# An attention and mixture-of-experts kernel: weight differences, token sums and outputs at other places

## Chip, core and metric

One core of a Trainium2 chip. The metric is the device time of one execution in microseconds (us). The engines are TensorE (PE; its weight loads, which overlap it, are PEld), VectorE (DVE), ScalarE (ACT), GpSimd (POOL) and SyncE (SP), which here only issues DMAs, all from one queue in order.

## The reference

Three stages over 4 x 576 = 2304 tokens: block-causal attention (8 heads of 64), an expert with h·cos(h), and eight experts with weights from eight rounds of normalisation. The groups of this change are those of the last stage:

```
def _moe2_ref(x, w_gate, w1, w2):          # x 2304x512, w1 8x512x1024, w2 8x1024x512
    logits = x @ w_gate; logits = logits - logits.max()
    P = np.exp(logits)
    for _ in range(8):
        P /= P.sum(1, keepdims=True) + 1e-09
        P /= P.sum(0, keepdims=True) + 1e-09
        P *= N / E
    for e in range(E):
        h = np.maximum(x @ w1[e], 0.0)
        out += P[:, e:e + 1] * (h @ w2[e])
    return out
```

## The kernel before

Every product in fp32 is made of three matmuls (`mm3`, L521 to L524) from "high" and "low" halves: a high half is a rounded copy (ScalarE), the low one the rest (VectorE or GpSimd subtracts the high half from the source). In the row names below, `xh`/`xl` and `wah`/`wal` are such halves.

The experts' stage works through 96 groups: three blocks of 768 tokens, in each 32 groups (8 experts by 4 slices of the hidden width). The first product of a group, x by a slice of w1, is made in seven products of sums of quarters instead of eight plain ones (the quarters' and sums' names are A11 to A22, S1 to S4 for one side, B11 to B22, T1 to T4 for the other). TensorE writes them to the PSUM tiles `hx`, `hy` and `hz`; copies and additions `c[0]`, `c[1]`, `c[2]` put them together.

*First block (groups 0 to 31).* These groups also make what the later blocks reuse. `wload` (L590) loads the slices of w1 and w2 of two groups on into two tiles `stg`. `Weights` then makes sums of w1's quarters on GpSimd (`s`, L603 to L606), high halves on ScalarE (L612, L613), low halves on VectorE (L617, L619), halves of w2 (`v`, ScalarE and GpSimd, L636, L637), and stores w1's halves to DRAM (L643). `differences` (L650) makes the four sums of quarters of w2 in place in `stg`, in two parts of two subtractions on VectorE, and the second part issues their store to DRAM (`td`, L654). In these groups the second product, h by w2, is six plain outputs (`y`, tile `acc`), one group later: y(0), y(1) behind product S3, y(2) to y(5) at the end. While groups 1 to 5 run, VectorE also makes the eight rounds of P (`plan`).

*Later blocks (groups 32 to 95).* Groups go in pairs (`Pair`, `pair_group`). The second product of a pair is made in seven products too: X1, Y1, X2, Z, X3, Y2, X4, each over three token tiles, 21 items. `TURN` is their order; X1 uses A11 by B11, Y1 uses S1 by T1, X2 uses S2 by T2, Z uses A12 by B21. `items(n)` runs n of them between the seven first products of the pair that follows. `high` (ScalarE) and `low` (L1113, VectorE) split the hidden side, `both` (L1122, L1125) makes its sums, `w2_split` (ScalarE L1077, GpSimd L1078) splits the side of the weights that came from DRAM. The six outputs of group 31 are made in group 32, in the slots of the pair that isn't there yet.

*The token sums.* `tprep` (L658) makes T1 to T4 of the next block: nine additions of 128 x 768 on GpSimd (L665), with T1's split in their middle; T2 to T4 are split in the last group of a block. `sums(n)` goes n steps further; it starts nine groups ahead of a block's end and goes on at each group's end, one step in even groups and two in odd ones.

The order on every engine is the order of the code.

Of the kernel before, what the change touches and what calls it, by code (L numbers as in the profile page):

```python
# [10 lines left out]
F32 = mybir.dt.float32  # L11
# [10 lines left out]
N, DM = B * S, H * D  # L22
# [4 lines left out]
TB = 384  # L27
# [5 lines left out]
NJ = F2 // 2  # L33
# [10 lines left out]
def attention_moe_kernel(ctx: ExitStack, tc: tile.TileContext, qk, v, w_a, gate, w_b, out):  # L44
    nc = tc.nc
# [26 lines left out]
    raw = [None] * F1  # L72
# [76 lines left out]
    post = ctx.enter_context(tc.tile_pool(name="post", bufs=2))  # L149
# [367 lines left out]
    with tc.manual_schedule():  # L517
# [53 lines left out]
        groups = [(tb, e, j) for tb in range(N // HB) for e in range(NE) for j in range(NJ)]  # L571
        NG, NA = len(groups), NE * NJ
        stg, wa, wv = {}, {}, {}
        drw = ctx.enter_context(tc.tile_pool(name="drw", bufs=1, space=bass.MemoryType.DRAM))
        W1D = [drw.tile([128, 14 * HK], F32, name=f"w1d{g}") for g in range(NA)]
        TD = [drw.tile([128, 4, 2, HK], F32, name=f"td{p}") for p in range(NA // 2)]
        PARTS = ((0, 3 * HK), (3 * HK, 3 * HK), (6 * HK, 4 * HK), (10 * HK, 4 * HK))
        th = tl = None

# [12 lines left out]
        class Weights:  # L592
# [40 lines left out]
            def v(self, i, eng=nc.gpsimd):  # L633
                src = stg[self.g][i][:, DM:2 * DM]
                t = wp.tile([128, 2 * DM], F32R, tag="w", name="wv")
                nc.scalar.activation(t[:, 0:DM], src, AF.Copy)  # L636
                eng.tensor_tensor(out=t[:, DM:2 * DM], in0=src, in1=t[:, 0:DM].bitcast(F32), op=ALU.subtract)  # L637
                wv[self.g, i] = t

            def store(self):  # L640

# [2 lines left out]

            def differences(self, part, eng=nc.vector):

                a, b = (t[:, DM:2 * DM] for t in stg[self.g])
                b11, b12, b21, b22 = a[:, 0:HK], a[:, HK:2 * HK], b[:, 0:HK], b[:, HK:2 * HK]
                for out, in0, in1 in (((b11, b12, b11), (b12, b12, b22)), ((b22, b22, b11), (b21, b21, b22)))[part]:
                    eng.tensor_tensor(out=out, in0=in0, in1=in1, op=ALU.subtract)  # L650
                if part:
                    p, k = divmod(self.g, 2)
                    for i, t in enumerate((a, b)):
                        nc.sync.dma_start(out=TD[p][:, 2 * i:2 * i + 2, k, :],  # L654
                                          in_=t.rearrange("p (o n) -> p o n", n=HK))
                    stg.pop(self.g)

        def tprep(tb, eng):  # L658

# [281 lines left out]
        fin = ctx.enter_context(tc.tile_pool(name="fin", bufs=1))  # L941
# [132 lines left out]
        def w2_split(p, o):  # L1074
            if (p, o) in W2:
                t, raw = W2[p, o], raws.pop((p, o))
                nc.scalar.activation(t[:, 0:DM], raw, AF.Copy)  # L1077
                nc.gpsimd.tensor_tensor(out=t[:, DM:2 * DM], in0=raw, in1=t[:, 0:DM].bitcast(F32), op=ALU.subtract)  # L1078
                w2_load(raw)
# [6 lines left out]
                ("Z", 0), ("Z", 1), ("X3", 0), ("X3", 1), ("X3", 2), ("Y2", 0), ("Y2", 1), ("Z", 2),  # L1086
                ("X4", 0), ("X4", 1), ("X4", 2), ("Y2", 2)]

        class Pair:


            def __init__(self, p):
                self.p = p
                self.tb, self.e, self.j = groups[2 * p]
                self.raw, self.h, self.l, self.bank, self.todo = {}, {}, {}, {}, list(TURN)

            def get(self, o, k=None):
                if o not in self.raw:
                    tag = places.pop(0)
                    self.raw[o] = tag, fin.tile([128, 2, TB], F32, tag=tag, name="raw")  # L1100
                r = self.raw[o][1]
                return r if k is None else r[:, k]

            def drop(self, o):
                places.append(self.raw.pop(o)[0])

            def high(self, o):
                self.h[o] = halves.pop(0)
# [54 lines left out]
                if self.e == NE - 1 and self.j == NJ - 2 and name in ("Y2", "X4"):  # L1163
                    nc.sync.dma_start(out=out[r * 128:(r + 1) * 128, :], in_=oa[r])

        def pair_group(g, old, new, splits, ys):

            k, now = g % 2, g < NG
            p = g // 2
            x = yy = c = None  # L1170

            def items(n):
                if old:
                    for _ in range(n):
                        old.multiply()
                elif k == 0:
                    for _ in range(n):
                        ys()

            if now:  # L1180
                c = [fin.tile([128, TB], F32, tag=f"c{i}", name="c") for i in range(3)]
# [13 lines left out]
            if old and k == 0:  # L1195
                old.low("S1")
                w2_split(p - 1, "B21")
            elif old:
                w2_split(p - 1, "T4")
            items(2)  # L1200
            if old and k == 0:
                old.both("S2", "A22", "S3", ALU.add)
# [32 lines left out]
                nc.vector.tensor_tensor(out=new.get("A22", k), in0=yy, in1=c[2], op=ALU.add)  # L1235
                splits("T3")
            if old and k == 0:
                old.low("A12")
            if now and k:
                new.low("A11", True)  # L1240
                w2_split(p, "T1")
            items(2)
            if now:
                product(g, x, "A22", "T4", False)
                nc.scalar.activation(new.get("A12", k), x, AF.Relu)
                splits("T4")
                if k:
                    new.relu("A22")
            if old and k == 0:
                old.high("S3")  # L1250
                old.high("S4")
                old.low("S3")
                w2_split(p - 1, "B22")
            items(1)
            if now:
                product(g, yy, "S4", "B22", False)
                nc.vector.tensor_tensor(out=new.get("A21", k), in0=yy, in1=c[1], op=ALU.add)
                if k:
                    new.high("A12")
                    w2_split(p, "T2")  # L1260
            items(2 - k)
            if now and k:
# [16 lines left out]
        tgen, at = None, ""  # L1279
        pairs = {}  # L1280
        used = {(2 * (NA - 1) + i) % 3 for i in range(2)}
        places = [f"hs{i}" for i in range(6) if i % 3 not in used]
        rest = list(range(2 * TT))

        def last_ys():
# [5 lines left out]
        for g in range(NG + 2):  # L1291
            now, w = g < NA, Weights(g + 1) if g + 1 < NA else None
            left = NE * NJ - g % (NE * NJ)
            if left == 9 and g + 9 < NG:
                tgen = tprep(groups[g + 9][0], nc.gpsimd)
                at = "sum"

            def sums(n):
# [10 lines left out]
            if g >= NA:  # L1309
                p = g // 2  # L1310
                if g == NA:
                    more = fin.tile([128, 4 * HK], F32, tag="s", name="s")
                    w2_load(more[:, 0:DM])
                    w2_load(more[:, DM:2 * DM])
                    w2_load(post.tile([128, S], F32, tag="lt", name="raw", bufs=1)[:, 0:DM])
                if 2 * p < NG and p not in pairs:
                    pairs[p] = Pair(p)
                pair_group(g, pairs.get(p - 1), pairs.get(p), splits, last_ys)
                sums(1 + g % 2)
                continue  # L1320

            def ys(t):
                if g:
                    y(g - 1, t)
# [5 lines left out]
            if now:  # L1330
# [23 lines left out]
                    w.lo_b()  # L1354
                product(g, x, "S3", "T3", False)
                gate("S3")
                Weights(g).differences(0)
                nc.scalar.activation(c[2], x, AF.Copy)
                nc.vector.tensor_tensor(out=c[2], in0=yy, in1=c[2], op=ALU.add)
                splits("T3")  # L1360
            ys(0)
            gate("y0")
            Weights(g).differences(1)
            if w and g:
                w.hi_a()
            ys(1)
# [28 lines left out]
            elif g == 0:  # L1395
                w0.store()
                w1.store()
            sums(1 + g % 2)
            ys(5)
            if g == NA - 1:  # L1400
                w1_tiles(g + 3, (0,))
# [31 lines left out]
```

## Time and profile before

| | before |
|---|---|
| median of 3 runs | 2097.68 us (2096.49 to 2098.88) |
| profiled execution: time / span | 2099.2 us / 2097.3 us |
| PE busy | 2067.8 us (99%), 12687 matmuls |
| PEld busy | 1944.3 us (93%) |
| DVE busy | 1573.7 us (75%) |
| ACT busy | 1046.8 us (50%) |
| POOL busy | 832.5 us (40%) |
| chain that ended last, by engine | PE 92%, DVE 5%, DMA 1%, issue 1%, ACT 1% |
| mean granted clock of PE | 0.995 |

The busy times are shares of the span and overlap. In the page's slices PE has 9 tenths or more everywhere but in the last one (8). A row such as "PE hx L522 <- ACT c L1343" in the waits reads: PE, about to write `hx` in line 522, waited for ScalarE's instruction of line 1343, which writes `c`.

### The profile page before, as it was taken

The numbers are of one execution on the slowest core, as the hardware profiler recorded it, in microseconds if no ns is written. First come the engines' busy times: TensorE is split into PE (matmuls) and PEld (weight loads), VectorE is DVE, ScalarE is ACT, GpSimd is POOL, SyncE is SP. The second block draws the span as 40 slices with busy tenths as digits, with TensorE's granted clock in tenths as the row PEclk, the third lists the DMA queues.
The fourth block names the chain that finished last, engine by engine and source line by source line (L and its number), as shares of the span: only waits on it lengthen the run. The fifth ranks groups of instructions, "written<-read, shape, count | busy, mean of one in ns | idle before, by whom it ended". The sixth has DMA issues, their size and how long they took to land.

```text
span 2097.3 us, 34781 instructions
## 1 busy us (share of the span) xinstructions
PE 2067.8 (99%) x12687; PEld 1944.3 (93%) x12687; DVE 1573.7 (75%) x2733; ACT 1046.8 (50%) x1852; POOL 832.5 (40%) x631
## 2 busy tenths in 40 slices
PE   9999999999999999999999999999999999999998
PEld 7888999999988888888888999999999999999998
DVE  7887886566768876777876777777887777777777
ACT  7887774343444434333433544554445445445443
POOL 4553232333324444344551333333553333333333
PEclk9999999999999999999999999999999999999999
DMA  6774320000025666666566555555455655555553
GB/s 167 185 186 133 108 91 1 6 11 31 1 106 196 205 226 217 210 228 215 206 218 235 170 197 182 197 180 184 165 178 182 206 203 173 187 201 179 191 174 111
DMA packets 176026, 337.75 MB, mean 161 GB/s; under 512 B 41936, under 2 KB 86480, under 8 KB 175856
## 3 DMA queue, kind: packets, MB, share of 16 engines
q1 hardware_dynamic: 175856, 335.54, 48.1%
q8 instruction: 100, 1.64, 0.3%
q14 instruction: 70, 0.57, 0.1%
HBM read 245.96 MB, written 80.36 MB: 156 GB/s over the span
## 4 chain that ended last, share of the span: by engine, by line
PE 92%; DVE 5%; DMA 1%; issue 1%; ACT 1%; POOL 0%; SPq 0%; DVEq 0%; ACTq 0%
PE acc L794 10%; PE p L524 7%; PE p L523 7%; PE p L522 7%; PE hx L522 6%; PE hx L523 6%; PE hx L524 6%; PE o L358 4%; PE acc L522 4%; PE acc L524 4%; PE acc L523 4%; PE h L522 3%; PE h L524 3%; PE h L523 3%; PE hy L522 3%; PE hy L523 3%
## 5 line engine op out<-in xcount | busy, mean ns | idle before, releaser
L1078 POOL TENSOR_TENSOR w<-s,w 128x512 fp32r<-128x512 f32 x150 | 237.3, 1582 | 418.7 <-ACT w L1077 399.4
L1162 DVE SCALAR_TENSOR_TENSOR oa<-p,P,oa 128x256 f32<-128x256 f32 x648 | 280.7, 477 | 66.2 <-PE p L524 64.4
L524 PE MATMUL p<-w,xl 128*128 128x256 f32 x894 | 253.9, 284 | 7.7 <-DVE xl L1113 7.7
L523 PE MATMUL p<-w,xh 128*128 128x256 f32 x834 | 235.0, 282 | 0.0
L522 PE MATMUL p<-w,xh 128*128 128x256 f32 x834 | 234.6, 281 | 0.0
L637 POOL TENSOR_TENSOR wv<-stg,wv 128x512 fp32r<-128x512 f32 x62 | 111.8, 1823 | 223.3 <-ACT wv L636 223.3
L1078 POOL TENSOR_TENSOR w<-raw,w 128x512 fp32r<-128x512 f32 x74 | 118.2, 1597 | 188.8 <-ACT w L1077 177.0
L524 PEld LDWEIGHTS p<-w,xl 128*128 128x128 f32 x894 | 170.6, 191 | 9.1 <-DVE xl L1113 8.9
L748 POOL TENSOR_TENSOR jl<-raw,jh 128x512 fp32r<-128x512 f32 x63 | 92.4, 1467 | 189.5 <-ACT jh L743 166.2
L523 PEld LDWEIGHTS p<-w,xh 128*128 128x128 f32 x834 | 158.1, 190 | 0.0
L522 PEld LDWEIGHTS p<-w,xh 128*128 128x128 f32 x834 | 157.7, 189 | 0.0
L522 PE MATMUL acc<-wv,hs 128*128 128x512 f32 x384 | 154.0, 401 | 0.9 <-DVE oa L1023 0.9
L524 PE MATMUL acc<-wv,hs 128*128 128x512 f32 x384 | 152.8, 398 | 0.0
L523 PE MATMUL acc<-wv,hs 128*128 128x512 f32 x384 | 152.5, 397 | 0.0
L522 PE MATMUL p<-w,xl 128*128 128x256 f32 x510 | 145.1, 284 | 1.0 <-ACT xl L1109 1.0
L523 PE MATMUL p<-w,xl 128*128 128x256 f32 x510 | 145.0, 284 | 0.0
L1029 DVE SCALAR_TENSOR_TENSOR oa<-acc,P,oa 128x512 f32<-128x512 f32 x168 | 122.7, 742 | 13.1 <-PE acc L524 12.8
L522 PE MATMUL hx<-th,w 128*128 128x384 f32 x384 | 129.5, 337 | 2.0 <-ACT c L1234 2.0
L523 PE MATMUL hx<-tl,w 128*128 128x384 f32 x384 | 128.9, 336 | 0.0
L524 PE MATMUL hx<-th,w 128*128 128x384 f32 x384 | 128.7, 335 | 0.0
L524 PE MATMUL p<-w,xh 128*128 128x256 f32 x450 | 127.8, 284 | 0.2 <-DVE xh L1113 0.2
L522 PE MATMUL h<-xh,jh 128*128 128x384 f32 x368 | 123.6, 336 | 0.0
(306 smaller groups left out, 6387.7 us busy)
## 6 DMA issues: line engine op xcount, KB each, us to landing
w<-w1d SPq DMA_DIRECT2D x128, 512.0 KB
w<-w1d SPq DMA_DIRECT2D x128, 384.0 KB
stg<-in_w_b_dram SPq DMA_DIRECT2D x64, 512.0 KB
s<-td SPq DMA_DIRECT2D x85, 256.0 KB
s<-in_w_b_dram SPq DMA_DIRECT2D x65, 256.0 KB
td<-stg SPq DMA_DIRECT2D x64, 256.0 KB
w1d<-wah SPq DMA_DIRECT2D x32, 512.0 KB
w1d<-wal SPq DMA_DIRECT2D x32, 512.0 KB
```

The costliest lines, as they stand in the source:

```text
L358: nc.tensor.matmul(o[:, q0:q1], vt[:, c], e, start=c == 0, stop=True, skip_group_check=c > 0)
L522: nc.tensor.matmul(ps, lh, rh, start=first, stop=False, skip_group_check=go_on)
L523: nc.tensor.matmul(ps, lh, rl, start=False, stop=False, skip_group_check=go_on)
L524: nc.tensor.matmul(ps, ll, rh, start=False, stop=last, skip_group_check=go_on)
L637: eng.tensor_tensor(out=t[:, DM:2 * DM], in0=src, in1=t[:, 0:DM].bitcast(F32), op=ALU.subtract)
L748: eng.tensor_tensor(out=lo, in0=raw[units[n][1]][:, part * DM:(part + 1) * DM], in1=hi.bitcast(F32), op=ALU.subtract)
L794: nc.tensor.matmul(acc[half, b][:, at:at + w_], w[:, s], h[:, t0:t0 + w_], start=f == 0 and i == 0 and at == 0, stop=f == F1 - 1 and i == ...
L1029: nc.vector.scalar_tensor_tensor(out=o, in0=acc, scalar=p, in1=o, op0=ALU.mult, op1=ALU.add)
L1078: nc.gpsimd.tensor_tensor(out=t[:, DM:2 * DM], in0=raw, in1=t[:, 0:DM].bitcast(F32), op=ALU.subtract)
L1162: nc.vector.scalar_tensor_tensor(out=o, in0=ps, scalar=p, in1=o, op0=ALU.mult, op1=ALU.add)
```

## The change

1. For groups 0 to 5 (`LATE`), `differences` leaves its two places in the group. `stg` is given free after `v`. From group 6 on, in every even group up to 16, `again` loads the w2 halves of one of these groups a second time (two DMAs of 256 KB), into tiles "tt"; the first part of its differences is made in the next group and the second part, with the store to DRAM, in the one after that, between y(4) and y(5).
2. `tprep` starts 14 groups ahead of a block's end instead of 9 and takes one step at a time: in the first block at the end of each group, as before; in pairs only in odd groups, once behind `w2_split` of T4 and once behind the `relu` of A22.
3. The six outputs of group 31: four in group 32 (in the slots of two), two in group 33 (in the slots behind S3 and behind T4). Two more places "tt" hold the raw tiles of the pair.
4. The items of the last pair come in another order (`LAST`): Z's first two directly behind X1, ahead of Y1. The low half of A12 is made in group 95, ahead of S1, and not behind it.

SyncE, the first groups; `stg` are the loads of w1 and w2, `w1d` and `td` the stores. Before:

```order
L590 DMA stg<-in_w_b_dram 128x1024 x4
L654 DMA td_2411<-stg 128x2x256 x2
L590 DMA stg<-in_w_b_dram 128x1024 x2
L643 DMA w1d_2379<-wbh 128x768
L643 DMA w1d_2379<-wbl 128x768
L643 DMA w1d_2379<-wah 128x1024
L643 DMA w1d_2379<-wal 128x1024
```

Now:

```order
L591 DMA stg<-in_w_b_dram 128x1024 x6
L646 DMA w1d_2379<-wbh 128x768
L646 DMA w1d_2379<-wbl 128x768
L646 DMA w1d_2379<-wah 128x1024
L646 DMA w1d_2379<-wal 128x1024
```

The store of the differences no longer stands between the loads.

GpSimd, the first two sums for the third block, `w` being low halves of w2's sides. Before (end of group 55):

```order
L1078 TENSOR_TENSOR w_15126<-raw,w_15126 128x512
L1078 TENSOR_TENSOR w_15127<-s,w_15127 128x512
L1078 TENSOR_TENSOR w_15128<-s,w_15128 128x512
L665 TENSOR_TENSOR tt<-xl 128x768
L665 TENSOR_TENSOR tt<-xh 128x768
L1078 TENSOR_TENSOR w_15129<-raw,w_15129 128x512
```

Now (group 51):

```order
L1089 TENSOR_TENSOR w_14308<-raw,w_14308 128x512
L676 TENSOR_TENSOR tt<-xl 128x768
L1089 TENSOR_TENSOR w_14480<-s,w_14480 128x512
L1089 TENSOR_TENSOR w_14481<-s,w_14481 128x512
L676 TENSOR_TENSOR tt<-xh 128x768
L1089 TENSOR_TENSOR w_14482<-raw,w_14482 128x512
```

The two sums, which stood together, have B11's and T1's splits between them.

VectorE, end of group 95 and start of the last pair's items; `oa` are the outputs' sums. Before:

```order
L1257 TENSOR_TENSOR raw<-hy,c 128x384
L1162 SCALAR_TENSOR_TENSOR oa<-p_21779,P,oa 128x256
L1122 SCALAR_TENSOR_TENSOR raw<-raw 128x768 x2
L1113 TENSOR_TENSOR xl<-raw,xl 128x768
```

Now:

```order
L1282 TENSOR_TENSOR raw<-hy,c 128x384
L1136 TENSOR_TENSOR xl<-raw,xh 128x768
L1185 SCALAR_TENSOR_TENSOR oa<-p_21803,P,oa 128x256
L1145 SCALAR_TENSOR_TENSOR raw<-raw 128x768 x2
L1136 TENSOR_TENSOR xl<-raw,xl 128x768
```

A12's low half (the second row) came in ahead of S1's sum and low half.

The diff, cut to its core:

```diff
+        LATE, late = 6, {}
...
                 wv[self.g, i] = t
+                if i == 1 and self.g < LATE:
+                    stg.pop(self.g)
...
-                a, b = (t[:, DM:2 * DM] for t in stg[self.g])
+                a, b = late[self.g] if self.g < LATE else (t[:, DM:2 * DM] for t in stg[self.g])
...
+            def again(self):
+                _, e, j = groups[self.g]
+                late[self.g] = [post.tile([128, 2 * TB], F32, tag="tt", name="w2", bufs=3)[:, 0:DM] for _ in range(2)]
+                for t, f in zip(late[self.g], (j, j + NJ)):
+                    nc.sync.dma_start(out=t, in_=w_b[e, f, :, DM:2 * DM])
...
+        LAST = [("X1", (0, 1, 2)), ("Z", (0, 1)), ("Y1", (0, 1, 2)), ("X2", (0, 1, 2)), ("Z", (2,)),
+                ("X3", (0, 1, 2)), ("Y2", (0, 1, 2)), ("X4", (0, 1, 2))]
...
+                if 2 * p + 2 == NG:
+                    self.todo = [(n, t) for n, ts in LAST for t in ts]
...
-            def items(n):
+            def items(n, fill=False):
                 if old:
                     for _ in range(n):
                         old.multiply()
-                elif k == 0:
-                    for _ in range(n):
-                        ys()
+                elif n == 2 if k == 0 else fill:
+                    ys()
...
                 w2_split(p - 1, "T4")
+                sums(1)
             items(2)
...
-                old.low("A12")
+                if "A12" not in old.l:
+                    old.low("A12")
             if now and k:
                 new.low("A11", True)
                 w2_split(p, "T1")
-            items(2)
+            items(2, True)
             if now:
                 product(g, x, "A22", "T4", False)
...
                     new.relu("A22")
+                    sums(1)
...
-            items(1)
+            items(1, True)
...
                     new.high("A12")
+                    if g == NG - 1:
+                        new.low("A12", True)
                     w2_split(p, "T2")
...
-        places = [f"hs{i}" for i in range(6) if i % 3 not in used]
+        places = [f"hs{i}" for i in range(6) if i % 3 not in used] + ["tt", "tt"]
...
-            if left == 9 and g + 9 < NG:
-                tgen = tprep(groups[g + 9][0], nc.gpsimd)
+            if left == 14 and g + left < NG:
+                tgen = tprep(groups[g + left][0], nc.gpsimd)
...
-                pair_group(g, pairs.get(p - 1), pairs.get(p), splits, last_ys)
-                sums(1 + g % 2)
+                pair_group(g, pairs.get(p - 1), pairs.get(p), splits, sums, last_ys)
...
-                Weights(g).differences(0)
+                if g >= LATE:
+                    Weights(g).differences(0)
...
-            Weights(g).differences(1)
+            if g >= LATE:
+                Weights(g).differences(1)
...
-            sums(1 + g % 2)
+            sums(1)
+            k = g - LATE
+            if k > 0 and (k - 1) // 2 < LATE:
+                Weights((k - 1) // 2).differences((k - 1) % 2)
+            if k % 2 == 0 and 0 <= k // 2 < LATE:
+                Weights(k // 2).again()
             ys(5)
```

## Rows read from the trace of the kernel before

**Rows 1.** TensorE's waits, 600 to 720 us: total, times, longest, in us.

```profile
PE hx L522 <- ACT c L1343: 5.2, 3, 2.1
PE acc L522 <- DVE oa L1023: 0.9, 2, 0.5
PE pcs L976 <- DVE sm L972: 0.9, 1, 0.9
PE hy L522 <- DVE c L1359: 0.8, 1, 0.8
```

**Rows 2.** Timeline of ScalarE: start, duration, instruction, idle before and its releaser.

```profile
613.78 0.49 ACT L1338 ACTIVATE c<-hx 128x384 f32<-128x384 f32 x1 [0.61 <-PE hx L524]
617.00 0.63 ACT L612 ACTIVATE wbh<-stg 128x512 fp32r<-128x512 f32 x1 [2.72 <-DMA stg<-in_w_b_dram]
...
707.09 0.49 ACT L1338 ACTIVATE c<-hx 128x384 f32<-128x384 f32 x1 [0.47 <-PE hx L524]
...
722.88 0.49 ACT L1338 ACTIVATE c<-hx 128x384 f32<-128x384 f32 x1 [3.53 <-PE hx L524]
```

**Rows 3.** Timeline of SyncE's queue, around 630 and 790 us.

```profile
625.62 5.55 SPq L654 DMA_DIRECT2D td<-stg  x2
631.27 0.90 SPq L590 DMA_DIRECT2D stg<-in_w_b_dram  x2
...
782.82 0.89 SPq L643 DMA_DIRECT2D w1d<-wal  x1
792.51 2.29 SPq L654 DMA_DIRECT2D td<-stg  x2
```

**Rows 4.** Windows: length, busy of each engine, PE's granted clock, DMA share, GB/s.

```profile
612.00:650.00 38.00, 33.84 (x158) 29.11 (x158) 28.48 (x55) 17.49 (x32) 17.09 (x14) 0.91 0.64 228
1500.00:1550.00 50.00, 46.05 (x303) 45.64 (x302) 42.28 (x57) 20.33 (x34) 26.47 (x14) 0.93 0.49 173
2077.00:2085.00 8.00, 7.80 (x39) 7.25 (x39) 7.42 (x13) 4.53 (x7) 5.11 (x4) 0.57 0.09 33
```

**Rows 5.** TensorE's waits, 720 to 1130 us; timelines of GpSimd and VectorE.

```profile
PE hy L522 <- DVE c L1359: 1.3, 2, 0.7
...
991.80 1.84 POOL L665 TENSOR_TENSOR tt<-xh 128x768 f32<-128x768 f32 x1
...
773.17 0.56 DVE L1351 TENSOR_TENSOR c<-hz,c 128x384 f32<-128x384 f32 x1 [3.21 <-PE hz L524]
...
777.65 0.87 DVE L650 TENSOR_TENSOR stg<-stg 128x256 f32<-128x256 f32 x2
```

**Rows 6.** TensorE's waits, 1400 to 1610 us; timelines of GpSimd and VectorE.

```profile
PE p L524 <- DVE xl L1113: 7.0, 4, 2.1
...
1471.83 2.54 POOL L665 TENSOR_TENSOR tt<-xh 128x768 f32<-128x768 f32 x1
...
1472.62 2.57 DVE L1113 TENSOR_TENSOR xl<-raw,xh 128x768 fp32r<-128x768 f32 x1
```

**Rows 7.** Timeline of GpSimd, the splits of B11 and T2 in one odd pair group.

```profile
1431.09 1.55 POOL L1078 TENSOR_TENSOR w<-s,w 128x512 fp32r<-128x512 f32 x1 [3.66 <-DMA w<-w1d]
...
1438.47 1.29 POOL L1078 TENSOR_TENSOR w<-s,w 128x512 fp32r<-128x512 f32 x1 [1.77 <-ACT w L1077]
```

**Rows 8.** TensorE's waits, 1130 to 1150 us; its timeline around one output.

```profile
PE hx L522 <- ACT c L1234: 1.8, 1, 1.8
...
1128.85 0.40 PE L522 MATMUL acc<-wv,hs 128*128 128x512 f32 x1
...
1130.25 0.34 PE L522 MATMUL hx<-th,w 128*128 128x384 f32 x1
```

**Rows 9.** TensorE's waits, 2060 to 2097 us; timelines of VectorE and GpSimd.

```profile
PE p L522 <- ACT xl L1109: 1.0, 1, 1.0
...
2075.76 0.96 DVE L1113 TENSOR_TENSOR xl<-raw,xl 128x768 fp32r<-128x768 f32 x1
...
2076.32 1.53 POOL L1078 TENSOR_TENSOR w<-s,w 128x512 fp32r<-128x512 f32 x1 [2.29 <-ACT w L1077]
```

More of the change, by code (lines that the diff above doesn't have):

```diff
@@ L655, in differences @@
                                           in_=t.rearrange("p (o n) -> p o n", n=HK))
-                    stg.pop(self.g)
+                    if self.g >= LATE:
+                        stg.pop(self.g)
+            def again(self):
[3 more added lines that the diff above has]
+                    nc.sync.dma_start(out=t, in_=w_b[e, f, :, DM:2 * DM])
         def tprep(tb, eng):
@@ L1099, in get @@
                     tag = places.pop(0)
-                    self.raw[o] = tag, fin.tile([128, 2, TB], F32, tag=tag, name="raw")
+                    if tag == "tt":
+                        t = post.tile([128, 2 * TB], F32, tag=tag, name="raw", bufs=3)
+                        t = t.rearrange("p (k n) -> p k n", n=TB)
+                    else:
+                        t = fin.tile([128, 2, TB], F32, tag=tag, name="raw")
+                    self.raw[o] = tag, t
                 r = self.raw[o][1]
@@ L1104, in drop @@
             def drop(self, o):
-                places.append(self.raw.pop(o)[0])
+                tag = self.raw.pop(o)[0]
+                if tag != "tt":
+                    places.append(tag)
             def high(self, o):
@@ L1164, in collect, with pair_group @@
                     nc.sync.dma_start(out=out[r * 128:(r + 1) * 128, :], in_=oa[r])
-        def pair_group(g, old, new, splits, ys):
+        def pair_group(g, old, new, splits, sums, ys):
             k, now = g % 2, g < NG
```

## The prediction

> **What bounds the kernel now.** The page's first part and its slices come first: TensorE is busy in nearly the whole of the span, in every slice (the table of the profile has it), and nothing that the change touches takes a product away. What can be won is therefore only what TensorE stands still for, and what its clock costs after it stood still. Second I read the list of TensorE's waits, cut into the stretches that the change touches; third, for each wait, the rows of the engine that ended it and of the engine or queue behind that; fourth, the granted clock of the same stretches.
>
> Groups 0 to 5 (600 to 720 us): four kinds of wait, 7.8 us together [rows 1], 5.2 of them for ScalarE's copy c[1] (L1343). ScalarE is not busy there: it stood 2.72 us for the landing of w_b before the high halves (L612) that are queued ahead of that copy [rows 2]. The load was late since SyncE's queue is in order: it stood 5.55 us in the store of the differences (L654), and only then issued the load (L590) of two groups on [rows 3]. The store itself waits for VectorE's differences. The copy c[0] opens each group: from 613.78 to 707.09 there are five groups in 93.31 us, where the next one alone takes 15.79 [rows 2]; so 93.31 − 5 × 15.79 = 14.4 us are lost, against 7.8 listed. The granted clock tells most of the rest: 0.91 over 38 us, and 0.09 × 38 = 3.4 us [rows 4]; in parts of this stretch TensorE ran at 1.2 instead of 2.4 GHz, behind its waits.
>
> Groups 23 and 27 are followed by waits of 1.3 us in two times for L1359 [rows 5], behind two token sums in a row on GpSimd (1.84 each). The first pair (from 1117 us): one wait of 1.8 us for the copy L1234 [rows 8]. Groups 55 to 62: four waits, 7.0 us, for VectorE's low half L1113, and a clock of 0.93 over 50 us, 3.5 us [rows 4, 6]. There the low half takes 2.57 us, beside a sum of 2.54 on GpSimd; the same form takes 0.96 with GpSimd free [rows 6, 9]. The end: a wait of 1.0 for the high half of S1 and a clock of 0.57 over the last 8 us, 3.4 us [rows 4, 9].
>
> **Part 1, six groups' differences go later.** From groups 0 to 5 go 4 × 6 subtractions on VectorE (two by 0.87 us where nothing is in the way [rows 5], so 1.7 a group) and 12 stores on SyncE. With no store ahead of it, the load for two groups on is issued as soon as its tiles are free; then the landing that ScalarE stood 2.72 us for comes before its need, and c[1] is not held up. VectorE, crowded by the softmax-like rounds of P in these groups, has 1.7 us a group less to do, which is more than its longest wait (0.9) [rows 1]. Late next is VectorE itself, which in groups 2 to 5 has little room left. I take all listed waits, 7.8, and the clock, 3.4. Of the 3.2 us between 11.2 and the 14.4 lost, a part is refilling of TensorE behind each wait, at most 3.2 / 7 = 0.45 a wait; I take 0.15, a third, since P's own small products are in it too: 7 × 0.15 = 1.1. **−12.3**, from −7 (the ScalarE and first VectorE waits without the clock) to −14.4.
>
> The work comes back in groups 6 to 18: 12 loads of 256 KB ahead of the same 12 stores, and 12 times one pair of subtractions between the last outputs. On VectorE a pair is 0.87, at a place behind which it idles 3.21 us before L1351 [rows 5]: hidden, 0. If that cover were gone it would cost up to 12 × 0.87 = 10.4. On SyncE two such loads take about as long to issue as those of rows 3, 0.90 us; the queue is moved ahead of nothing else until the next load for two groups on. Between the group's last store of w1 (ends at 782.82 + 0.89 = 783.71) and its next instruction (792.51) it has 8.8 us free [rows 3]: 0. The 12 × 0.25 = 3 MB more to read land in the same gaps. 0 for the whole, from 0 to +10.4; no gain is possible, as these groups show no wait for VectorE's differences now.
>
> **Part 2, the sums of T1 to T4 are spread.** First block: one sum at the end of every group instead of one or two. The waits behind the pairs of sums go, 1.3 and twice 0.15 of refilling: **−1.6**, from 0 to −1.6. Third block's sums: the pair of sums at the end of odd groups stood on GpSimd just when VectorE had S1's pieces and low half to make. The new places, one behind T4's split and one behind T1's, lie where GpSimd idles 3.66 and 1.77 us before its next split [rows 7]. A sum alone is 1.84 [rows 5], so the first place hides it, and the second makes T2's split 0.07 late, which VectorE and TensorE don't feel: the product T2 is used later. What is hidden there costs 0.1 to 1.8 if the hole is gone. The seven or so VectorE operations of two inputs around the new places may now be the ones to be held; no row shows that, and I bound it by the waits of today: it gives back between 0 and all 7.0. TensorE waits 7.0 and clock 3.4 to 3.5 go (I take 3.4), with 4 × 0.15 refilling: **−11.0**, from 0 to −11.1. The split of T1 in the middle of the sums comes earlier with them: one low half of 0.96 [rows 9], 0 to +1, taken as 0.
>
> **Part 3, the outputs of the last ordinary group are spread over the first pair.** Between S3 and T4 in group 33 there is nothing now while ScalarE copies, and TensorE waits 1.8. One output is put there: six matmuls from 1128.85 to 1130.25, 1.40 us [rows 8]. 0.4 stays: **−1.4**, from 0 (the outputs taken from group 32 uncover a like copy there) to −1.8.
>
> **Part 4, another order at the end.** Before, Y1 follows X1 and waits for S1's halves; the low one ends at 2075.76 + 0.96 = 2076.72 [rows 9]. Now Z follows X1, and Z needs B21, whose high half on ScalarE stands behind S1's, and whose low half on GpSimd ends at 2076.32 + 1.53 = 2077.85 before [rows 9]. And A12's low half (0.96) is now ahead of S1 on VectorE; since an operation of this kind and GpSimd's don't run beside each other [rows 6], it pushes T2's split and S1 by some of that: I take 0.6 of 0.96. So 2078.45 against 2076.72, 1.7 later, less 0.2 for waits inside Y1 that its later place ends: **+1.5**. The clock there cost 3.4; it may be spared or paid twice, so from −1.9 to +4.9.
>
> **A rule of the skill.** The low half took 2.57 us beside GpSimd's sum and 0.96 without it [rows 6, 9]. The Trainium skill, SBUF — State Buffer, "Who interferes with whom", says that a VectorE instruction with two SBUF inputs and a GpSimd instruction that reads SBUF lock each other out for a whole instruction, and that the one issued first has it. The trace agrees: the sum has 1.75 us to go when the low half starts, and 1.75 + 0.96 is near 2.57. It speaks for part 2 and against part 1: the moved pairs of subtractions, two SBUF inputs each, land at the end of a group beside GpSimd's splits and its sums of the next weights. By it GpSimd could be late in 12 groups, and the time 2083.1 instead of 2072.9; that is rival 1.
>
> **The sum.** −12.3 − 1.6 − 11.0 − 1.4 + 1.5 = −24.8. The profiled execution has a span of 2097.3 us and took 2099.2; 2099.2 − 24.8 = 2074.4. It stands 1.5 above the median of the runs, 2097.68, so the median after is 2072.9.
>
> **Rivals.** *1: the late differences make a new wait.* In groups 7 to 18 they push GpSimd's sums onto VectorE's low halves, as the pair of sums does behind groups 23 and 27: 0.7 and 0.15 each time [rows 5], 12 × 0.85 = 10.2 given back, **2083.1**. For it: the same engines and the same place in the group. Against: one sum at that place, in the groups between, leaves no wait, and 0.87 is half of a sum.
>
> *2: VectorE is the bound in groups 2 to 5 even without the differences.* Then the ScalarE waits go and others take their place; half of part 1, 6.2, stays away: **2079.1**. For it: three of the four kinds of wait there are VectorE's [rows 1]. Against: 1.7 us a group less work.
>
> *3, slower: SyncE's queue blocks again, in groups 6 to 18.* The second of the two loads writes a tile that the store just ahead of it still reads, so the queue stands until that store has landed, and the load for two groups on stands behind it. If that load is late as it was in groups 1 and 2, each of the six groups with a load pays what those two paid, (7.8 + 3.4) / 2 = 5.6: 33.6 given back, **2106.5**. It decides from 24.8 / 6 = 4.1 us a group. Against: 8.8 us free in the queue [rows 3], where a stay of 5.55 was the longest there.
>
> *4: part 2 doesn't do what it says:* the sums in the new places hold VectorE as much as in the old ones. −11.0 is not won: **2083.9**. For it: 2.5 us of exclusive work in a pair's group stays. Against: idle times of 3.66 and 1.77 [rows 7].
>
> **How the numbers follow.** Forecast 0.68; rival 1 0.10; rival 2 0.09; rival 4 0.06; rival 3 0.05; several at once, near no change, 0.02. The predicted time is 2072.9. The range goes down by the bounds of parts 1 and 4 (2.1 and 3.4, not both in full) to 2068, and up over rivals 1, 2 and 4 to 2085. Faster by over 0.2%, about 4 us and about what a measurement of this kernel can tell from no change: 0.93; within: 0.02; slower: 0.05.
>
> **What would show it.** Right: in 600 to 720 us no wait for L1343's copy and c[0] copies about 16 us apart; SyncE never over 2 us in one instruction there; no wait for L1359 after groups 23 and 27; in the third block's sums the low half at about 1 us, no wait over 0.5 and a clock of 1.00 there; in the last pair a wait of Z for the split of B21 (ScalarE, then GpSimd) in place of that of Y1. Wrong: waits for L1359 in groups 7 to 18 (rival 1), VectorE's waits in groups 2 to 5 (rival 2), ScalarE's for w_b in groups 8 to 20 (rival 3), VectorE's low halves of 2.5 us beside sums (rival 4).

## The result, and the profile after

The changed kernel took 2071.07 us (median of four runs, 2069.90 to 2072.07) against 2097.09; the ratio is 0.9874, 95% interval [0.9857, 0.9892]: 26 us faster. The forecast was 2072.9 us, in a range of 2068 to 2085. The profiled execution has a span of 2068.1 us (before: 2097.3) and lasted 2069.9.

The waits of [rows 1, 5, 6, 8] are gone, but for one of 0.4. TensorE's waits after, 600 to 720 us: none. From 720 to 1130 us (total, times, longest):

```profile
PE hx L522 <- ACT c L1257: 0.4, 1, 0.4
```

From 1400 to 1610 us:

```profile
PE hy L522 <- DVE raw L1282: 0.7, 1, 0.7
PE hx L522 <- ACT c L1257: 0.2, 1, 0.2
```

From 2040 us on:

```profile
PE p L522 <- ACT w L1088: 2.1, 1, 2.1
PE p L523 <- POOL w L1089: 1.2, 1, 1.2
```

The first is what is left of part 3's 1.8 us, the middle two stood in the kernel before as well (last group of the second block), the last two are the new waits of part 4: Z for the halves of B21. The windows that answer to [rows 4], with the granted clock third from the end:

```profile
612.00:650.00 38.00, 38.00 (x196) 34.21 (x196) 27.28 (x60) 21.02 (x41) 18.68 (x16) 1.00 0.53 188
1500.00:1550.00 50.00, 50.00 (x357) 50.00 (x357) 38.69 (x65) 25.58 (x42) 21.56 (x14) 1.00 0.57 198
2048.00:2060.00 12.00, 10.79 (x78) 10.59 (x79) 10.90 (x22) 4.73 (x7) 6.19 (x4) 0.86 0.07 22
```

TensorE is busy in all of the first two stretches and its clock stays at 2.4 GHz, where it had 0.91 and 0.93. In the first groups ScalarE's high halves (L613, before: L612) now follow the copy c[0] (L1364, before: L1338) at once, and c[1] (L1369) waits for nothing but TensorE; compare [rows 2], where ScalarE stood 2.72 us for the landing. The five groups that [rows 2] count from copy c[0] to copy c[0] take 16.2 us each (612.56 to 693.56), against 18.7 before; the two behind them, without P's work, take 15.72 each.

```profile
612.56 0.49 ACT L1364 ACTIVATE c<-hx 128x384 f32<-128x384 f32 x1 [0.61 <-PE hx L524]
612.94 0.62 ACT L613 ACTIVATE wbh<-stg 128x512 fp32r<-128x512 f32 x1
...
614.64 0.49 ACT L1369 ACTIVATE c<-hx 128x384 f32<-128x384 f32 x1 [0.76 <-PE hx L524]
```

Where the gain came from, in the two profiled executions: for part 1 the copies c[0] tell it. Seven groups take 124.8 us before (613.78 to 738.60) and 112.4 after (612.56 to 725.0), and the way to the first of them is 0.8 shorter. For the other parts I add up by how much the distance from one matmul to the next exceeds what is usual for its shape: the stretches with groups 23 and 27 lose 2.0 us before and 0.1 after; 1120 to 1160 us 2.7 and 0.7; 1440 to 1600 us 12.7 and 1.5; the last pair 5.6 and 5.2. That is −13.2, −1.9, −2.0, −11.2 and −0.4 where −12.3, −1.6, −1.4, −11.0 and +1.5 were forecast. Together it is 28.7 of the 29.2 us between the two spans; the start of the program, which the change doesn't touch, differs by 0.4.

### The profile page after: what moved, and what is told of

It reads as the page before. It is cut to its first block, busy times and chain, and to the rows that moved or that the text cites. A ratio compares the mean times of both kernels' runs of the same rounds, so it can differ in the third digit from the quotient of the medians.

```text
span 2068.1 us, 34730 instructions
## 1 busy us (share of the span) xinstructions
PE 2054.9 (99%) x12687; PEld 1936.6 (94%) x12687; DVE 1551.5 (75%) x2733; ACT 1045.1 (51%) x1852; POOL 824.7 (40%) x631
## 4 chain that ended last, share of the span: by engine, by line
PE 66%; issue 24%; POOL 8%; DMA 1%; ACT 0%; DVE 0%; POOLq 0%; SPq 0%; DVEq 0%; ACTq 0%
PE acc L805 7%; POOL w L1089 6%; PE acc L522 4%; PE acc L524 4%; PE acc L523 4%; PE o L358 4%; PE hx L522 4%; PE hx L524 4%; PE hx L523 4%; PE p L523 3%; PE p L524 3%; PE p L522 3%; PE h L522 2%; PE h L524 2%; PE h L523 2%
## 5 line engine op out<-in xcount | busy, mean ns | idle before, releaser
L524 PE MATMUL p<-w,xl 128*128 128x256 f32 x906 | 255.8, 282 | 0.0
L522 PE MATMUL p<-w,xh 128*128 128x256 f32 x846 | 238.1, 281 | 2.1 <-ACT w L1088 2.1
L523 PE MATMUL p<-w,xh 128*128 128x256 f32 x846 | 238.8, 282 | 1.2 <-POOL w L1089 1.2
L638 POOL TENSOR_TENSOR wv<-stg,wv 128x512 fp32r<-128x512 f32 x62 | 111.0, 1810 | 231.3 <-ACT wv L637 224.2
L522 PEld LDWEIGHTS p<-w,xh 128*128 128x128 f32 x846 | 160.0, 189 | 2.3 <-ACT w L1088 2.3
L523 PEld LDWEIGHTS p<-w,xh 128*128 128x128 f32 x846 | 160.5, 190 | 1.4 <-POOL w L1089 1.4
L523 PE MATMUL p<-w,xl 128*128 128x256 f32 x498 | 140.0, 281 | 0.0
L522 PE MATMUL p<-w,xl 128*128 128x256 f32 x498 | 139.8, 281 | 0.0
L1132 ACT ACTIVATE xh<-raw 128x768 fp32r<-128x768 f32 x141 | 117.6, 842 | 18.1 <-DVE raw L1145 7.7
```

The costliest lines, as they stand in the source:

```text
L522: nc.tensor.matmul(ps, lh, rh, start=first, stop=False, skip_group_check=go_on)
L523: nc.tensor.matmul(ps, lh, rl, start=False, stop=False, skip_group_check=go_on)
L524: nc.tensor.matmul(ps, ll, rh, start=False, stop=last, skip_group_check=go_on)
L1132: nc.scalar.activation(self.h[o], self.get(o), AF.Copy)
```

## The experiments

Kernels of one list below ran on one chip; differences to the changed kernel go by the ratios to the kernel before on the same chip. The changed kernel has 0.9874, and 0.9868 when it ran again, whence two numbers for a difference.

**Parts undone.** First part 1:

```diff
-        LATE, late = 6, {}
+        LATE, late = 0, {}
```

> The changed kernel with part 1 undone: all 32 groups make and store their differences in their own group again; parts 2 to 4 stay. Theory (the store ahead of the load on SyncE's queue holds ScalarE's high halves up, and VectorE has room without the differences): the four kinds of wait and the half clock of 600 to 720 us come back, +12.3 us against the changed kernel, near 2083.4, the waits again 5.2 for ScalarE's c[1] and some 2.6 for VectorE. Rival (the gain there came from something else in the change): under +4. If the late differences cost something in groups 7 to 18, as rival 1 said, the gain of leaving them there shows as less than +12.3.

2084.59 us, ratio 0.9934 [0.9921, 0.9948]: 12.6 to 13.8 above the changed kernel. TensorE's waits, 600 to 720 us, are those of [rows 1] again:

```profile
PE hx L522 <- ACT c L1369: 5.6, 3, 2.2
PE hy L522 <- DVE c L1386: 1.0, 2, 0.8
PE acc L522 <- DVE oa L1034: 1.0, 2, 0.5
PE pcs L987 <- DVE sm L983: 0.9, 1, 0.9
```

Part 1 as a whole is worth what the term said; a cost of the moved differences in groups 6 to 18 would show as less than 12.3, and none does.

Part 2 undone (start at `left == 9`, `sums(1 + g % 2)` at the groups' ends, the two calls in `pair_group` removed):

> The changed kernel with part 2 undone: the token sums start nine groups ahead of a block's end and go on at the groups' ends, one step in even and two in odd groups. Theory: the waits for L1359's addition behind groups 23 and 27 (1.3 us and refilling) and the four waits for the low half of S1 with the half clock behind two of them (11.0) come back: +12.6 us, near 2083.7. Rival (the old places would do no harm in the shifted order of the pairs): under +4.

2084.07 us, 0.9930 [0.9918, 0.9943]: 11.7 to 13.0 above. The waits are those of [rows 5, 6] again, 1.3 us in two times and 7.0 in four. The theory, +12.6, is confirmed.

Part 4 undone (`TURN` for the last pair too, no early low half of A12), and beside it a try to mend part 4:

```diff
-                    w2_split(p, "T2")
+                    w2_split(p, "B21" if g == NG - 1 else "T2")
...
-                w2_split(p - 1, "B21")
+                w2_split(p - 1, "B21" if now else "T2")
```

> The changed kernel with part 4 undone: the last pair's items in the order of all other pairs, A12's low half behind S1 again. By the prediction's term part 4 costs 1.5 us, so this one would be 1.5 faster, near 2069.6. By the two traces the last stretch, waits and clock together, came out about 0.4 us better with the new order (waits 1.7 longer, the stretch at half clock shorter): then +0.4, near 2071.5, which these runs will hardly tell from nothing. The trace will tell: waits of 1.0 and 0.5 for S1's halves and a clock near 0.57 for 8 us behind them, against 3.3 of waits and 0.62 for 4 us.

> The changed kernel with B21's split (ScalarE, then GpSimd) in the place of T2's in group 95, and T2's in the place of B21's, ahead of the last items. Theory (Z, now second in the last pair, waits 2.1 + 1.2 us for the two halves of B21, which stand behind S1's high half on ScalarE): GpSimd ends B21's low half about when X1 ends, both waits go and with them most of the half clock behind them, 3.3 + 1.7 = 5.0 us: near 2066. Rival (Y1 or X2 meet the same wait one step later, for S1's or T2's halves): no change, near 2071.

Old order: 2069.22 us, 0.9860 [0.9847, 0.9874], 1.7 to 2.9 below the changed kernel by the ratios. B21 first: 2070.35, 0.9867 [0.9854, 0.9881], no difference; the theory (5.0 us faster) fell. TensorE's waits at the end of this one:

```profile
PE p L522 <- DVE oa L1185: 1.7, 1, 1.7
PE p L524 <- DVE xl L1136: 1.0, 2, 0.5
PE p L522 <- ACT xh L1132: 0.8, 1, 0.8
```

The two waits for B21 are gone, the clock was 1.00 from 2048 to 2060 us, and yet nothing was won: TensorE, now at full speed, waits 3.5 us further on for VectorE (`oa`, low halves) and for a high half behind it. VectorE was busy for 11.72 of those 12 us, so the rival (the same wait one step later) was right.

**On a second chip:** the changed kernel again, a second try at the end, part 3 undone, and a test of part 1's cause. The second try splits T2 only together with B21, so that GpSimd is idle while VectorE makes S1 and S3 (and keeps the old order of the items):

```diff
                 if k:
                     new.high("A12")
-                    if g == NG - 1:
-                        new.low("A12", True)
-                    w2_split(p, "T2")
+                    if g < NG - 1:
+                        w2_split(p, "T2")
...
                 old.low("S1")
+                if not now:
+                    w2_split(p - 1, "T2")
                 w2_split(p - 1, "B21")
```

> The changed kernel itself, beside the others of this call, so that parts and last order are compared on one chip. Expected 2071 within 1.5. If part 4 costs what the prediction said (1.5), it lies above the kernel with the old last order by that, as the medians so far have it (2071.07 against 2069.22).

> Part 4 undone (old order of the last items), and T2's split in the last pair made together with B21's, behind S1's halves, so that GpSimd is idle while VectorE makes S1 and S3. Theory: the two sums took 2.66 us beside GpSimd's split of T2 where two such take 1.9, so S1's high half and with it Y1 come 0.7 to 0.9 earlier: the wait of 1.0 falls to about 0.2 and that of 0.5 goes, 1.3 us; if TensorE's clock then stays at 2.4 GHz, up to 3.4 more, less what VectorE's later pieces take back as waits: near 2067.5, from 2065 to 2069. Rival (VectorE, over 95% busy in the last 20 us, is the bound of the whole stretch, and a wait taken away comes back a piece later): within 1 us of 2069.2.

> The changed kernel with part 3 undone: all six outputs of group 31 in group 32 again. Theory: the wait of 1.8 us for ScalarE's copy between S3 and T4 in group 33 comes back, +1.4 by the prediction's term and +2.0 by the excess of TensorE's spacing in the two traces (2.7 against 0.7 in 1120 to 1160 us): near 2072.8. Rival (the outputs in group 32 covered as much): 0.

Again: 2070.71 us, 0.9868 [0.9854, 0.9881]. T2 later: 2072.83, 0.9874 [0.9859, 0.9889]; not better. Its waits at the end:

```profile
PE p L524 <- DVE xh L1134: 2.5, 1, 2.5
PE p L522 <- ACT xl L1130: 1.0, 2, 0.8
PE p L524 <- DVE xl L1134: 0.5, 1, 0.5
```

The first half of the theory came true: the wait for S1's high half, 1.0 in the old order, is 0.2 here (its two sums take 1.82 us). But behind it stand one of 0.8 and one of 2.5 for the halves of the next sums, which VectorE now makes beside the splits that were put off (2.89 us for two sums, 2.02 for a low half). Moving the splits only moved the place where VectorE is waited for. Part 3 undone: 2073.28 us, 0.9878, 2.1 to 2.6 above the changed kernel of the same chip, with the wait of 1.8 back, as in [rows 8]; the intervals of the two overlap, so the trace carries this more than the times.

```profile
PE hx L522 <- ACT c L1258: 1.8, 1, 1.8
```

Then the cause of part 1's gain. At the places where groups 0 to 5 had their differences, VectorE makes four subtractions of the same size on a spare tile; no load or store hangs on them.

```diff
+            def busy():
+                if not spare:
+                    spare.append(post.tile([128, 2 * TB], F32, tag="tt", name="busy", bufs=3))
+                    nc.vector.memset(spare[0], 0.0)
+                t = spare[0]
+                for _ in range(2):
+                    nc.vector.tensor_tensor(out=t[:, 0:HK], in0=t[:, HK:2 * HK], in1=t[:, 2 * HK:3 * HK],
+                                            op=ALU.subtract)
```

> The changed kernel with four subtractions of 128x256 in each of groups 0 to 5 at the places where the differences stood, on a tile that nothing else uses: VectorE is as busy there as in the kernel before, but no store and no load hangs on it. Theory (the gain of part 1 is the load that came late behind the differences and their store): only VectorE's own waits come back, at most 0.9 + 0.9 + 0.8 = 2.6 and no half clock: 2071 to 2074. Rival (VectorE had no room, and its 1.7 us a group are the gain): +6 to +12, 2077 to 2083.

2081.11 us, 0.9918 [0.9905, 0.9930]: 10.4 above the changed kernel, and so my theory fell. No wait for ScalarE came back, but one kind for VectorE's addition c (L1398), 6.1 us in four, and 0.83 of the clock in 600 to 620 us. TensorE's waits:

```profile
PE hy L522 <- DVE c L1398: 6.1, 4, 1.8
```

One of the four, 1.8 us, is in group 0, where GpSimd has nothing beside it: a fill of 0.70 us, which only the experiment has, and a pair of 0.89 stand ahead of the addition. The low clock follows this wait, where the kernel before has 0.8 us of wait and a clock of 1.00. So about half of the 10.4, the 5.2 us lost by 620 us, is in part the experiment's own. The other three waits, 4.3 us, are in groups 2 to 4. VectorE's timeline at one of them:

```profile
639.58 3.10 DVE L1359 TENSOR_TENSOR busy<-busy 128x256 f32<-128x256 f32 x2
642.60 0.55 DVE L1398 TENSOR_TENSOR c<-hy,c 128x384 f32<-128x384 f32 x1
```

GpSimd's at the same place:

```profile
639.54 2.39 POOL L629 TENSOR_TENSOR wal<-s,wah 128x1024 fp32r<-128x1024 f32 x1 [1.57 <-PE pcs L987]
```

The pair of subtractions takes 3.10 us and not 0.87, beside GpSimd's low half, which began 0.04 us ahead of it. The addition for which TensorE waits stands behind this pair. In the kernel before, with the late load, GpSimd's low half of the same group began later and met the group's second pair, with the addition (643.32) already done. VectorE's row, then GpSimd's:

```profile
646.70 3.04 DVE L650 TENSOR_TENSOR stg<-stg 128x256 f32<-128x256 f32 x2
646.59 2.41 POOL L628 TENSOR_TENSOR wal<-s,wah 128x1024 fp32r<-128x1024 f32 x1 [4.26 <-PE hx L524]
```

**On a third chip:** is that VectorE's own load, or the two engines keeping each other out? Fills, which read nothing, in place of those subtractions (`nc.vector.memset(t[:, 0:2 * HK], 0.0)`):

> As the kernel with the added subtractions in groups 0 to 5 (2081.1), but with fills of 128x512 on VectorE in their place, which last about as long (a fill of 128x768 took 0.70 there, a subtraction 0.44) and read nothing. In that kernel a pair took 3.1 us instead of 0.87 where GpSimd's low half L629 (2.4 us) ran beside it. Theory now: not VectorE's own work is what costs, but that subtractions with two inputs in SBUF and GpSimd's work keep each other out; then the fills cost at most the first group's wait: 2070 to 2075. Rival (VectorE has simply no room for 1.8 us more a group): near 2081 again.

2078.36 us, 0.9905 [0.9890, 0.9920]: between the two, and above the 2075 that the theory allowed. TensorE's waits:

```profile
PE hy L522 <- DVE c L1397: 2.1, 1, 2.1
PE pcs L987 <- DVE sm L983: 0.4, 1, 0.4
```

The same place on VectorE:

```profile
640.39 0.48 DVE L1359 MEMSET busy<- 128x512 f32 x1
641.05 0.48 DVE L1359 MEMSET busy<- 128x512 f32 x1 [0.17 <-DVE busy L1359]
641.45 0.49 DVE L1397 TENSOR_TENSOR c<-hy,c 128x384 f32<-128x384 f32 x1
```

And on GpSimd:

```profile
640.22 2.40 POOL L629 TENSOR_TENSOR wal<-s,wah 128x1024 fp32r<-128x1024 f32 x1 [2.58 <-PE pcs L987]
```

In groups 2 to 4 the waits for the addition are gone, though VectorE has as many instructions and GpSimd's low half stands beside them: there it was the two inputs, not the number of instructions. What stays is group 0: one wait of 2.1 us and a clock of 0.91 in 600 to 640 us, which is VectorE's own time, with the first fill of 0.7 us in it. By the distances between matmuls, 640 to 680 us lost 5.2 with subtractions and 0.3 with fills, 600 to 640 us 5.4 and 6.0.

Fills in place of the sums, now on GpSimd and in the old places of part 2 (the third block's T1 to T4 are zero then):

```diff
+                if tb == 2:
+                    for _ in range(2):
+                        eng.memset(out, 0.0)
+                    return
                 eng.tensor_tensor(out=out, in0=in0, in1=in1, op=what)
```

> The changed kernel with the third block's token sums back in the old places (one at the end of even, two at the end of odd groups from nine groups ahead), but each sum replaced by two fills of 128x768 on GpSimd, about 1.8 us together; what the sums compute is left out, so the third block's T1 to T4 are zero. Theory (a sum keeps VectorE's operations with two SBUF inputs out for as long as it reads): the fills don't, the low half of S1 takes 0.96, the four waits of 7.0 us don't come: within 1 us of the changed kernel, 2071. Rival (GpSimd is busy too long there and its splits come late, or any GpSimd work holds VectorE): +6 to +11, 2077 to 2082.

2072.32 us, 0.9877 [0.9861, 0.9894]. Of 7.0 us in four waits 0.5 in one is left. That wait, then GpSimd's timeline at the first place, to be held against [rows 6]:

```profile
PE p L524 <- DVE xl L1140: 0.5, 1, 0.5
...
1451.91 3.03 POOL L678 MEMSET tt<- 128x768 f32 x4
```

VectorE's:

```profile
1453.71 0.96 DVE L1140 TENSOR_TENSOR xl<-raw,xh 128x768 fp32r<-128x768 f32 x1
```

GpSimd is busy at the same place, for 3.0 us instead of 2 × 2.54, and the low half takes 0.96 us, not 2.57. Four fills are shorter than two sums that are held up themselves (two undisturbed ones take 3.7), but the low half lies wholly beside them. So it is the reading that holds VectorE, not that GpSimd is busy.

Last the two covers on which the cost of nothing in groups 6 to 18 rested. Each late load issued twice, and each late subtraction made three times:

```diff
-                    nc.sync.dma_start(out=t, in_=w_b[e, f, :, DM:2 * DM])
+                    for _ in range(2):
+                        nc.sync.dma_start(out=t, in_=w_b[e, f, :, DM:2 * DM])
```

> The changed kernel with each of the 12 late loads of w2 issued twice, the second time into the same tile. In the changed kernel SyncE's queue was taken from 738.17 to 746.10 by one store and one pair of loads, since the second load stands until the store ahead has landed, and the next store fell due at 747.32: 1.2 us are left, not the 8 that the prediction counted on. Theory (rival 3's mechanism is real, and only those 1.2 us keep it off): each second load stands for the first one's landing, some 2 to 6 us, the load for two groups on is late by 1 to 5 us in six groups, and ScalarE's high halves and TensorE wait: +3 to +30. Rival (the load has more slack than the queue): 0, 2071.

> The changed kernel with every late subtraction made three times in place (the values of six groups' differences are wrong then), 12 times 1.74 us more on VectorE between y(4) and y(5). VectorE idled 3.2 us behind that place, 1.97 after the change. Theory (that idle time is the cover): 1.74 fits just into it, 0 to +3. Rival 1's mechanism (the moved subtractions run beside GpSimd's sums and push L1386's addition): 12 x 0.85 or more, +10 and over.

Loads twice: 2080.69 us, 0.9919 [0.9905, 0.9934], 9.4 to 10.7 above. The theory held. ScalarE's c[1] is waited for again, and ScalarE stands for the landing of w_b again (1.85 and 1.92 us in two groups looked at):

```profile
PE hx L522 <- ACT c L1370: 8.5, 5, 2.4
```

SyncE's queue in the changed kernel:

```profile
738.17 3.45 SPq L657 DMA_DIRECT2D td<-w  x2
741.67 4.43 SPq L667 DMA_DIRECT2D w<-in_w_b_dram  x2
747.32 2.29 SPq L657 DMA_DIRECT2D td<-stg  x2
```

In this one:

```profile
741.59 3.89 SPq L657 DMA_DIRECT2D td<-w  x2
745.53 8.65 SPq L668 DMA_DIRECT2D w<-in_w_b_dram  x4
754.27 0.90 SPq L657 DMA_DIRECT2D td<-stg  x2
```

In the changed kernel the queue is through at 746.10, and the next store falls due at 747.32, 1.2 us later. With the loads doubled it stands until 754.18, some 3.5 us after that store is due by the same distances. So rival 3's mechanism (a queue that stands too long makes the load for two groups on late) is real, and 1.2 us kept it off.

Subtractions three times: 2084.77 us, 0.9936 [0.9921, 0.9950], 13.0 to 14.3 above; the theory, 0 to +3, fell, and it is rival 1's mechanism, at more than its 10.2. TensorE's waits, 720 to 930 us, 12 times:

```profile
PE hy L522 <- DVE c L1387: 9.3, 12, 1.1
```

VectorE's timeline at one of the late places:

```profile
740.92 2.19 DVE L654 TENSOR_TENSOR w<-w,w 128x256 f32<-128x256 f32 x3
743.14 2.60 DVE L654 TENSOR_TENSOR w<-w 128x256 f32<-128x256 f32 x3
```

GpSimd's sums beside it (two of four):

```profile
741.95 0.88 POOL L604 TENSOR_TENSOR s<-stg 128x256 f32<-128x256 f32 x1 [0.46 <-DMA stg<-in_w_b_dram]
742.79 0.91 POOL L605 TENSOR_TENSOR s<-stg 128x256 f32<-128x256 f32 x1
```

Six subtractions take 4.79 us, not 6 × 0.44: those beside GpSimd's work take 0.85 each, and one of GpSimd's instructions ends between each two (the last four end at 743.11, 743.99, 744.87 and 745.75 us, GpSimd's at 742.82, 743.70, 744.59 and 745.46). In the changed kernel a late pair takes 1.28 (0.85 and 0.43) in three of the 12 groups, with 1.96 of the idle time left behind it, and 1.7 to 1.8 in eight, with about 1.5 left. In the last, beside the first token sum of part 2, it takes 2.8, and 0.43 is left. The first and the last:

```profile
724.20 0.85 DVE L653 TENSOR_TENSOR w<-w 128x256 f32<-128x256 f32 x1
725.08 0.43 DVE L653 TENSOR_TENSOR w<-w,w 128x256 f32<-128x256 f32 x1
...
728.13 0.56 DVE L1377 TENSOR_TENSOR c<-hz,c 128x384 f32<-128x384 f32 x1 [1.96 <-PE hz L524]
...
897.11 0.85 DVE L653 TENSOR_TENSOR w<-w,w 128x256 f32<-128x256 f32 x1
898.00 1.96 DVE L653 TENSOR_TENSOR w<-w 128x256 f32<-128x256 f32 x1
...
901.05 0.56 DVE L1377 TENSOR_TENSOR c<-hz,c 128x384 f32<-128x384 f32 x1 [0.43 <-PE hz L524]
```

## Why the prediction was right, point by point

**Part 1, −12.3: the size right, the cause half right.** Undone, it gave 12.6 to 13.8. The chain told (store, load, high halves, c[1]) was what the trace of before showed and what came back when the part was undone. But the text gave VectorE's relief only 2.6 us of it, and that step failed: with the load free and VectorE's subtractions left, 10.4 of the 12 to 13 us came back. About half of that (groups 2 to 4) is new: the early load brings GpSimd's low half forward, onto the pair of subtractions ahead of the addition c. The other half (group 0 and the low clock behind it) is VectorE's own time and holds the experiment's fill, so 10.4 is more than the relief is worth; how much more stays open. Rival 2's condition (VectorE is the bound there as soon as its load stays) is shown at least for groups 2 to 4; in the changed kernel the subtractions are gone, and it doesn't arise. The 1.7 us a group that the text took for VectorE's relief holds where nothing runs beside: in groups 1 and 2 of the kernel before the two pairs took 4.6 and 3.9 us, beside GpSimd. What moving the store alone would win wasn't tried, nor whether the load could go ahead of the differences in a kernel that keeps them in place, since they read the tile that the load overwrites.

One sign that was named didn't hold: SyncE stood over 2 us in 600 to 720 us. The second of two loads waited for GpSimd's half of w2 (`wv`, L638), which frees the tile. TensorE waited for nothing on it:

```profile
610.83 6.55 SPq L591 DMA_DIRECT2D stg<-in_w_b_dram  x2
```

**The moved work, 0: right, with less room than the text said.** The 0.90 us for the two loads was the step that was mis-sized: store and loads hold the queue for 7.9 us of the 8.8. The second half of the store stands about 2.5 us for the late subtractions (16.7 us in six such stores), and the second load 3.3 us for the store's landing (16.6 in five); the sum left both out, although rival 3 named the second. Of the cover of 3.21 on VectorE between 1.96 and 0.43 was left, since a pair costs 1.28 to 2.8 beside GpSimd and not 0.87. That nothing came of it is in part luck: no term held these margins.

**Part 2, −11.0 and −1.6: right.** 11.7 to 13.0 by undoing it; in the new places the sums collided with nothing that TensorE waits for. Rival 4 is out. The fills show the cause, which had only been read from two durations.

**Part 3, −1.4: 2.0 by the distances between matmuls, 2.1 to 2.6 by undoing it.** The wait left is 0.4, as reckoned; the refilling of TensorE behind the wait, which was counted in the other parts, and a wait of 0.2 that went with it were not in the term.

**Part 4, +1.5: the direction likely right, the size nearer half, not settled.** The new waits are 2.1 + 1.2 us against 1.0 + 0.5 + 0.2, 1.6 longer, by the path told (S1's high half, then B21's on ScalarE, then GpSimd). The kernel without it was 1.7 to 2.9 faster, but the intervals overlap. The clock differs between executions of one and the same kernel: 0.86 from 2048 to 2060 us in the first profile of the changed kernel, 0.72 in the second, 1.7 us apart:

```profile
2048.00:2060.00 12.00, 9.81 (x57) 9.61 (x58) 9.81 (x18) 5.65 (x9) 5.58 (x4) 0.72 0.13 41
```

That is why the first pair of traces alone showed −0.4. More traces help. From the last `hx` product to the end of the span, the ten traces with the new order (the changed kernel twice, and eight experiments that leave the end as it is) take 27.3 to 28.7 us, median 28.3. The two with the old order (the kernel before, and the one with part 4 undone) take 27.5 and 27.7. By these the new order costs about 0.7. VectorE seems to be what bounds the end, whichever order the items have (11.72 of 12 us busy with B21 first); no run took work off VectorE there, so this is argued and not shown. The text took it for ScalarE's and GpSimd's order.

**The sum.** −24.8 forecast, −26.0 measured; the parts undone one by one give 23.5 to 27.7 in sum, so nothing large is left over. The kernel with the old last order, 2069.22, is the fastest that ran, and not separated from the changed one.

Rival 1, which didn't come, was weighed by a rule of the Trainium skill, SBUF — State Buffer, "Who interferes with whom": a VectorE instruction with two SBUF inputs contends with a GpSimd instruction that reads SBUF, and not with one that only writes it. The rows shown here agree: a pair of subtractions beside GpSimd's subtraction took 3.10 instead of 0.87, and a low half beside GpSimd's fills 0.96. A fill of VectorE's, which reads nothing, took 0.48 beside GpSimd's subtraction as well as alone.

## What to carry to other kernels

When a load comes early, look at which engine's work it brings forward and what that meets; here the cure for a late load made a new wait as soon as VectorE kept its subtractions. For work that is moved "into idle time", count the queue's stay until a landing and the other engine's instructions beside it, and double the work once to see how much room is left. When one engine is busy through a whole tail, reordering around it may only move the wait, as both tries did here.

## What was not expected of the hardware

A string of short VectorE instructions of two inputs took turns with GpSimd's, so that it paid for each of GpSimd's in between: six of 0.44 us took 4.79. And the stretch that TensorE spends at 1.2 GHz behind the same waits (2.1 and 1.2 us) lost 1.7 us in one execution of the changed kernel and 3.4 in another.
